# A 192-byte constant tile ahead of three load slots in a decode-attention kernel

## The chip, the core and the metric

The kernel runs on one core of a Trainium2 chip. The metric is the device time of one execution in microseconds. Over three runs it is 684.03 us in the median (683.95 to 684.05).

## The reference

One decode step: eight requests (B = 8), one new token each, model width D = 512. There are 32 query heads, 8 key/value heads and a cache of 4096 positions with 128 elements a head. All data is float32.

```python
xn = _layernorm(x, axis=-1)
...
q = (x @ wq).reshape(B, Sq, Hq, Dh).transpose(0, 2, 1, 3)
scores = jnp.einsum("bhqd,bhkd->bhqk", q, k) * (Dh ** -0.5)
p = _softmax(scores, axis=-1)
o = jnp.einsum("bhqk,bhkd->bhqd", p, v)
s = o.transpose(0, 2, 1, 3).reshape(B, Sq, Hq * Dh) @ wo
...
z = _gelu(jnp.einsum("bsd,df->bsf", x, w_in))
z1 = z[..., :Fh]
z2 = _layernorm(z[..., Fh:], axis=-1)
g = jnp.einsum("ts,bsf->btf", w_sp, z2) + b_sp[None, :, None]
g = _silu(jnp.einsum("bsf,fd->bsd", z1 * g, w_out))
...
return x + s * g
```

In both branches `x` is the normalized `xn`. K and V together are 8 x 8 x 4096 x 128 x 4 x 2 bytes, 268 MB, and each byte is used once; with the weights the kernel reads about 291 MB.

## The kernel before

Everything that is loaded in bulk goes through a **ring of three slots**, the pool `ring` (line 53, `slot()` at line 59). A slot is a tile of 128 partitions x 16384 float32, so 65,536 bytes of each partition and 8 MiB in all. The pools are opened in the order `const`, `ring`, `work`, `small`, and lie in SBUF in this order from low addresses up: first the small constant tiles, then the three slots, then the working tiles `p` and `pT` and the small ones. Where a slot begins therefore depends on how many bytes the constant tiles take.

The order of the work is written out by hand, and one queue, SyncE's (`nc.sync.dma_start`), carries all bulk loads in the order of the program:

- `w_mlp` (L70), the weights of the second branch, 38,912 bytes a partition, into the first slot, with three small pieces of w_out (L75) behind it in the same slot, in 8, 16 and 32 rows;
- `wq` (L86), a whole slot;
- for each of the 8 key/value heads: two loads of K (`load_k`, L313; half the requests each) and two of V (`load_v`, L320), each a whole slot. On the host K and V have been laid out so that each partition's 65,536 bytes are one contiguous run in HBM;
- for the last head, `wo` in seven pieces (L324) into one slot, and the last V in two halves.

A load into a slot waits until the engines are done with what the slot held before and until that earlier load has landed. With three slots, one is being used while two are loaded or wait to be.

The engines do this: `mlp()` computes the second branch into `gate`; `project_q()` (L236) makes the queries, spread with zeros into `qz`; then for each head `scores()` (L258) multiplies the slots with K by `qz` into the PSUM tile `sc`, 64 matmuls of 512 columns a slot; `softmax()` (L263 to L290) makes `pT`; `values()` (L300) multiplies the slots with V, again 64 matmuls a slot, and VectorE (L303, L305) takes the diagonal blocks; `combine()` (L309) gathers the head's output in `oT`. At the end `folded_wo()` (L331) and `direct_wo()` (L338) multiply by wo as its pieces land, two VectorE operations (L382, L383) apply gate and residual, and L384 stores the result, 128 rows of 512 bytes.

Of the kernel before, what the change touches and what calls it, by code (L numbers as in the profile page):

```python
# [8 lines left out]
F32 = mybir.dt.float32  # L9
# [4 lines left out]
P = 128  # L14
# [28 lines left out]
LOW_COLS = 10 * D  # L43
HL_AT = [0, 0, 8]
HL_CH = 10


@with_exitstack
def tile_gqa_gmlp_decode(ctx: ExitStack, tc: tile.TileContext, x, side, kT, v, wq, wo,
                         w_mlp, lows, out):  # L50
    nc = tc.nc
    const = ctx.enter_context(tc.tile_pool(name="const", bufs=1))
# [2 lines left out]
    small = ctx.enter_context(tc.tile_pool(name="small", bufs=2))  # L55
    ps_fix = ctx.enter_context(tc.tile_pool(name="ps_fix", bufs=1, space=bass.MemoryType.PSUM))
    ps = ctx.enter_context(tc.tile_pool(name="ps", bufs=2, space=bass.MemoryType.PSUM))

    def slot():
        return ring.tile([P, SLOT], F32, name="slot")  # L60
# [19 lines left out]
    def from_slot(rows, n):  # L80
        lo = spare[0]
        spare[0] = lo + n
        return mlp_slot[:rows, lo:lo + n]
# [57 lines left out]
    def mlp():  # L141
# [3 lines left out]
        hT = hy[:, :2 * P].rearrange("p (a s) -> p a s", a=2)  # L145
        hL = from_slot(P, HL_CH * P).rearrange("p (a s) -> p a s", s=P)
        y_sb, e = zu[:, :2].rearrange("p a f -> p (a f)"), zu[:, 2, :P]
# [282 lines left out]
```

## Time and profile before

| | |
|---|---|
| time, median of 3 runs | 684.03 us |
| time of the profiled execution | 683.97 us |
| its span, first to last instruction | 682.2 us |
| bytes moved | 291.22 MB in 6445 packets |
| mean rate over the span | 427 GB/s |
| granted TensorE clock, mean | 0.756 of full speed |

Times in the profile are microseconds from the span's start. L258 is line 258 of the kernel before. PE is TensorE's matmuls, PEld its weight loads, DVE VectorE, ACT ScalarE, POOL GpSimd, SP SyncE. The page cuts the span in 40 equal slices: in the row "DMA" each digit is the busy share of the 16 DMA engines in tenths (9 is 90% or more), and "GB/s" is what they moved. A packet is one unit of work of a DMA engine; the row of a queue gives packets, MB, and the packets' time as a share of 16 engines' span. The chain is followed back from the last instruction, at each step to what released it; told in order of time, its columns are start, length, and the work.

### The profile page before, as it was taken

To read this page: it belongs to the slowest core of one execution; us is meant where nothing else is said; L and a number is where in the kernel's file an instruction comes from. 1 tells how busy PE (TensorE), PEld (TensorE's weight loads), DVE (VectorE), ACT (ScalarE), POOL (GpSimd) and SP (SyncE) were. 2 spreads that over 40 slices of the span, in tenths; PEclk is the share of its full clock that TensorE was granted. 3 is DMA by queue.
4 is the path that set the end of the run, shared out by engine and by line. 5 is a ranking of instruction groups with operands and counts; after the bars stand their busy time and mean duration, and the time that the engine had idled before them with its cause. 6 is when DMAs were issued, how large, how long until landed. Compare 5 with 4: busy or idle time off the path is not lost.

```text
span 682.2 us, 5712 instructions
## 1 busy us (share of the span) xinstructions
PE 382.8 (56%) x2610; PEld 117.5 (17%) x2610; DVE 170.5 (25%) x272; ACT 13.5 (2%) x27; POOL 3.9 (1%) x11
## 2 busy tenths in 40 slices
PE   1488454456655355556754465655755356655666
PEld 0222121112111021111211021111211021111212
DVE  2531033401431024401431024401422024400432
ACT  0000000000000000000000000000000000000000
POOL 1000000000000000000000000000000000000000
PEclk9778667878767678887676678877667778876688
DMA  9999999999999999999999999999999999999996
GB/s 384 439 447 432 434 431 430 428 434 428 438 435 430 431 430 435 438 428 430 428 434 443 427 439 439 431 434 431 430 431 430 430 431 428 430 431 434 424 422 263
DMA packets 6445, 291.22 MB, mean 427 GB/s; under 512 B 726, under 2 KB 982, under 8 KB 1534
## 3 DMA queue, kind: packets, MB, share of 16 engines
q1 hardware_dynamic: 6262, 290.79, 98.8%
q8 instruction: 20, 0.33, 0.2%
q10 hardware_dynamic: 160, 0.08, 0.1%
q14 instruction: 3, 0.02, 0.0%
HBM read 290.80 MB, written 0.07 MB: 426 GB/s over the span
## 4 chain that ended last, share of the span: by engine, by line
DMA 79%; PE 16%; issue 4%; DVE 1%; POOLq 0%; POOL 0%
DMA slot<-in_kT 40%; DMA slot<-in_v 28%; DMA slot<-in_wo 10%; PE sc L258 8%; PE o_ps L300 6%; PE sc L215 1%; PE scr L201 0%; PE po_ps L309 0%; DMA x_sb<-in_x 0%; DVE zu L218 0%; DVE st L129 0%; PE scr L191 0%; POOLq L424 0%; POOL rstd L132 0%; PE sc L338 0%
## 5 line engine op out<-in xcount | busy, mean ns | idle before, releaser
L258 PE MATMUL sc<-slot,qz 128*32 128x512 f32 x1024 | 148.0, 743 | 132.1 <-DMA slot<-in_kT 132.1
L300 PE MATMUL o_ps<-slot,pT 128*16 128x512 f32 x1024 | 154.0, 744 | 77.8 <-DMA slot<-in_v 77.8
L303 DVE TENSOR_TENSOR o_all<-o_ps,diag 128x512 f32<-128x512 f32 x64 | 44.2, 691 | 156.7 <-PE o_ps L300 156.3
L263 DVE TENSOR_REDUCE nm<-sc 128x1 f32<-128x1024 f32 x8 | 9.8, 1224 | 278.7 <-PE sc L258 278.7
L258 PEld LDWEIGHTS sc<-slot,qz 128*32 128x32 f32 x1024 | 36.5, 133 | 237.3 <-DMA slot<-in_kT 138.1
L305 DVE TENSOR_REDUCE o_sb<-o_all 128x128 f32<-128x512 f32 x64 | 67.8, 1059 | 2.2
L300 PEld LDWEIGHTS o_ps<-slot,pT 128*16 128x16 f32 x1024 | 30.5, 113 | 161.6 <-issue 106.9
L309 PE MATMUL po_ps<-fold,o_sb 128*128 128x4 f32 x128 | 24.6, 263 | 24.1 <-DVE o_sb L305 23.8
L309 PEld LDWEIGHTS po_ps<-fold,o_sb 128*128 128x128 f32 x128 | 19.0, 188 | 68.8 <-DVE o_sb L305 65.5
L289 PE MATMUL scr<-ident,p 128*128 128x128 f32 x64 | 15.4, 422 | 10.7 <-DVE p L284 10.7
L265 ACT ACTIVATE p<-sc,nm 128x1024 f32<-128x1024 f32 x8 | 8.9, 1113 | 574.5 <-DVE nm L263 574.5
L289 PEld LDWEIGHTS scr<-ident,p 128*128 128x128 f32 x64 | 12.4, 221 | 11.1 <-issue 11.1
L290 DVE COPY pT<-scr 128x512 f32<-128x512 f32 x16 | 11.1, 691 | 11.3 <-PE scr L289 11.3
L155 PE MATMUL scr<-slot,xnT 128*32 128x256 f32 (+1 forms) x64 | 5.2, 464 | 9.5 <-DMA slot<-in_w_mlp 9.5
L236 PE MATMUL scr<-slot,xnT 128*32 128x512 f32 x64 | 9.4, 737 | 0.0
L268 PE MATMUL scr<-ident,nm 128*1 128x128 f32 x8 | 2.2, 270 | 10.9 <-DVE nm L263 10.9
L281 PE MATMUL scr<-wl,same 128*128 128x1 f32 x16 | 3.8, 309 | 6.2 <-DVE wl L279 6.2
L284 DVE TENSOR_SCALAR p<-p,w 128x1024 f32<-128x1024 f32 x8 | 6.0, 753 | 0.3
L331 PE MATMUL sc<-slot,oT 128*8 128x512 f32 x48 | 5.7, 593 | 0.2 <-DMA slot<-in_wo 0.2
L215 PE MATMUL sc<-slot 16*32 16x512 f32 (+2 forms) x36 | 5.3, 664 | 0.8 <-DVE zu L218 0.8
L171 PE MATMUL scr<-part_sum,same 128*128 128x1 f32 x4 | 1.1, 348 | 7.0 <-DVE part_sum L169 7.0
L155 PEld LDWEIGHTS scr<-slot,xnT 128*32 128x32 f32 x64 | 3.0, 141 | 11.3 <-issue 10.8
(87 smaller groups left out, 72.3 us busy)
## 6 DMA issues: line engine op xcount, KB each, us to landing
slot<-in_v SPq DMA_DIRECT2D x2, 4096.0 KB, 26.3
slot<-in_w_mlp SPq DMA_DIRECT2D x1, 4864.0 KB, 14.5
slot<-in_wo SPq DMA_DIRECT2D x1, 3072.0 KB, 36.5
slot<-in_wo SPq DMA_DIRECT2D x1, 2048.0 KB, 40.1
slot<-in_wo SPq DMA_DIRECT2D x1, 1280.0 KB, 42.7
slot<-in_wo SPq DMA_DIRECT2D x1, 768.0 KB
slot<-in_wo SPq DMA_DIRECT2D x1, 512.0 KB
slot<-in_wo SPq DMA_DIRECT2D x2, 256.0 KB, 31.8
```

The lines of the kernel that those rows point to most:

```text
L155: nc.tensor.matmul(pz[R * g:R * (g + 1), part * FQ:part * FQ + n], xnT[:, k, :], w_in_sb[:, k, part * FH + lo:part * FH + lo + n], start=( ...
L215: nc.tensor.matmul(sc[R * g:R * (g + 1), bank, :], lhsT, rhs, start=(i < G), stop=(i + G >= len(part)))
L236: nc.tensor.matmul(pq[R * g:R * (g + 1), :], xnT[:, k, :], wq_sb[:, k, lo:lo + REP * DH], start=(k == 0), stop=(k == NK - 1))
L258: nc.tensor.matmul(sc[R * g:R * (g + 1), c, :], qz[:, h, b * R:(b + 1) * R], k_sb[:, i, c, g, :], start=(b == 0), stop=(b == B - 1))
L263: nc.vector.tensor_reduce(m, sc, op=ALU.max, axis=AX.XY, negate=True)
L265: nc.scalar.activation(p.rearrange("p j s -> p (j s)"), sc.rearrange("p c s -> p (c s)"), AF.Exp, bias=m, accum_out=l[:, h:h + 1])
L289: nc.tensor.transpose(t[:, j * P:(j + 1) * P], p[:, 4 * c + j, :], ident)
L290: nc.vector.tensor_copy(pT[:, :, 4 * c:4 * c + 4].rearrange("p b j (g r) -> p (j g) b r", g=G), t.rearrange("p (m b r) -> p m b r", b=B, r ...
L300: nc.tensor.matmul(of[R * c:R * c + G * REP, :], pT[:, b, j, :], v_unit[:, j], start=(j < G), stop=(j >= J - G))
L303: nc.vector.tensor_mul(o_all, o, diag[:, :, None].to_broadcast([P, G, DH]))
L305: nc.vector.tensor_reduce(o_sb, o_all.rearrange("p g d -> p d g"), op=ALU.add, axis=AX.X)
L309: nc.tensor.matmul(po[:, b * REP:(b + 1) * REP], o_sb, fold, start=True, stop=True)
```

## The change

A constant tile of 128 partitions x 48 float32, 192 bytes a partition, is taken from the pool `const` ahead of all others. Nothing writes or reads it.

```diff
 HL_AT = [0, 0, 8]
 HL_CH = 10
+ALIGN = 48
...
     ps = ctx.enter_context(tc.tile_pool(name="ps", bufs=2, space=bass.MemoryType.PSUM))
+
+    const.tile([P, ALIGN], F32, name="align")
 
     def slot():
         return ring.tile([P, SLOT], F32, name="slot")
```

In the compiled programs the addresses of the tiles within a partition are these (bytes):

| tile | before | after | remainder by 512, before and after |
|---|---|---|---|
| x_sb, the first constant tile | 1152 | 1344 | 128, 320 |
| qz | 4800 | 4992 | 192, 384 |
| res | 16192 | 16384 | 320, 0 |
| first slot | 16704 | 16896 | 320, 0 |
| second slot | 82240 | 82432 | 320, 0 |
| third slot | 147776 | 147968 | 320, 0 |
| pT | 213312 | 213504 | 320, 0 |
| p | 217408 | 217600 | 320, 0 |

All other SBUF tiles of the kernel move by the same 192 bytes. The kernel's lines after the new ones have numbers three higher than before.

## The prediction

> **What bounds the kernel now.** I read the head of the page first, then the DMA lines and the chain that ended last, to see whether any engine matters at all.
>
> ```profile
> span 682.2 us, 5712 instructions
> ...
> PE 382.8 (56%) x2610; PEld 117.5 (17%) x2610; DVE 170.5 (25%) x272; ACT 13.5 (2%) x27; POOL 3.9 (1%) x11
> ...
> DMA  9999999999999999999999999999999999999996
> GB/s 384 439 447 432 434 431 430 428 434 428 438 435 430 431 430 435 438 428 430 428 434 443 427 439 439 431 434 431 430 431 430 430 431 428 430 431 434 424 422 263
> ...
> q1 hardware_dynamic: 6262, 290.79, 98.8%
> ...
> DMA 79%; PE 16%; issue 4%; DVE 1%; POOLq 0%; POOL 0%
> ```
>
> The busiest engine works 56% of the span, while the queue q1, on which SyncE's transfers run, keeps the 16 DMA engines busy for 98.8% of it. The rate is flat from the second slice to the last but one. So the time is the time of moving 290.79 MB. The page's chain gives PE 16% all the same; the chain in order of time, of the middle of the run and of its end, shows why that isn't PE's price:
>
> ```profile
> 78.35 9.60 PE sc L258 x64
> 87.94 0.02 issue
> 87.96 48.40 DMA slot<-in_kT
> 136.36 0.04 issue
> 136.40 9.58 PE sc L258 x64
> 145.99 0.02 issue
> 146.00 48.41 DMA slot<-in_v
> 194.41 0.04 issue
> ...
> 204.89 47.58 DMA slot<-in_v
> 252.47 0.14 issue
> ...
> 262.98 47.54 DMA slot<-in_kT
> 310.52 0.04 issue
> ```
>
> The first column is the start, the second the length. Each time the 64 matmuls on a slot end, the load that was waiting for that slot is issued, and lands 48.4 us later. The landings at the ends of the DMA rows are 136.36, 194.41, 252.47, 310.52: 58.05 us apart, whatever PE did between. The ring has three slots, so three loads of 8 MiB (8,388,608 bytes) land in 58.05 us: **19.35 us a load**, 433.5 GB/s. Of the 48.4 us from issue to landing only 19.35 are the load's own; in the other 29 us it queues behind two earlier loads. PE could give a slot back up to 29 us later and the queue would never run dry. What the chain puts down to PE is hidden behind the other two slots. At the end:
>
> ```profile
> 646.82 31.85 DMA slot<-in_wo
> 678.66 0.04 issue
> 678.71 0.45 PE sc L338 x8
> 679.16 0.02 issue
> 679.18 0.30 DVE res L382
> 679.48 0.02 issue
> 679.51 0.29 DVE res L383
> ```
>
> The last bytes of wo land at 678.66, and 3.5 us of small work and the store of the result follow to the span's end at 682.2. So any change in the time has to come out of the loads, or out of these 3.5 us.
>
> **The change, part by part.** The new tile is never read or written. The two compiled programs hold the same 1855 instructions in the same order on each engine with the same waits, and HBM tensors and PSUM tiles are where they were. Only SBUF addresses differ: all tiles of the kernel move up by 192 bytes. The three slots go from 16704, 82240 and 147776 (each 320 past a multiple of 512, 64 past one of 256) to 16896, 82432 and 147968 (multiples of 512). Nothing changes its distance to another tile. So there is no term for instructions, waits or queues: 0 us each. Two terms are left.
>
> *Engines reading and writing at shifted addresses.* A tile 64-byte-aligned before still is, and one that was not still isn't, since 192 is three times 64. No row shows an operation at both phases, so I bound it: a matmul on a slot could cost more or less, but for 29 us per slot it is covered, which is three times the 9.6 us that PE spends on one. Uncovered are the 0.45 us of L338, and 0.30 and 0.29 us of L382 and L383. If each were a tenth slower or faster, that is 0.1 us. I take 0.
>
> *The loads themselves.* How much of a row's time could depend on where the row starts? The packet counts say what a row is: the 42 big loads (w_mlp, wq, 16 of kT, 17 of v, 7 of wo) and the store have 128 rows each, 5504; the three low pieces of w_out have 8, 16 and 32 rows; that is 5560 of q1's 6262, and the 702 left are the small packets that close a transfer, 16 for each of the 43 (688) and 14 for the low pieces. So **one packet is one row of one partition**, and each of the 16 engines carries 42 x 128 / 16 = 336 rows of the big loads. A row is one contiguous run, so alignment can act at its two ends and otherwise only if every step inside is slower. The DMA lines of two windows tell the two apart, the first (140 to 300 us) of 64 KiB rows, the second (672 to 677 us) of the short rows of wo:
>
> ```profile
> q1 hardware_dynamic: 1183, 69.14, 99.9%
> ```
>
> ```profile
> q1 hardware_dynamic: 460, 1.54, 76.6%
> ```
>
> Packets, MB, share of 16 engines. The first is 0.999 x 160 x 16 = 2557.4 us of engine time, the second 0.766 x 5 x 16 = 61.3 us. With a fixed cost c for each packet and a rate r along it: 2557.4 = 1183 c + 69.14 MB / r and 61.3 = 460 c + 1.54 MB / r. That gives **c = 10 ns** (9.5 to 10.4 with the rounding of the 1.54) and r = 27.16 bytes per ns, 434.6 GB/s for 16 engines. So of a 64 KiB row's 2.42 us all but 10 ns goes at a steady rate.
>
> Alignment's part of the 10 ns is not in this trace, since every big load has the same phase. From above: all of it, 336 x 10 ns = 3.4 us saved, which leaves 680.6. From below: nothing saved, or a loss; I put the end of a loss at the same size, another 10 ns, +3.4 us. The nearest row with another phase at its destination is the store at the end, whose rows of 512 bytes go to an HBM tensor of 512-byte rows (window 680 us to the end, and the issue row):
>
> ```profile
> q1 hardware_dynamic: 144, 0.07, 10.1%
> ...
> out<-res SPq DMA_DIRECT2D x1, 64.0 KB, 1.5
> ```
>
> 0.101 x 2.2 x 16 = 3.56 us; less 65,536 / 27.16 = 2.41 us it leaves 1.14 us for 144 packets, **7.9 ns** a packet. It writes the other way, so it is a neighbour and no measurement; but a fixed cost of 8 ns where the destination starts on 512 leaves 2 ns of the 10 for the phase. I take the middle of 0 and 2 ns: 336 x 1 ns = 0.34 us.
>
> [...]
>
> **The sum.** The profiled execution took 683.97 us with a span of 682.2; the median of the three runs is 684.03 (683.95 to 684.05), 0.06 above it. 683.97 - 0.34 - 0 = **683.6 us**. A measurement of this kernel can tell about 0.2% from no change, 1.4 us, so this is no change: the limits are 682.66 and 685.40. In rows, 1.37 us / 336 = 4.1 ns: alignment has to be worth four of the ten nanoseconds to be seen.
>
> **Rivals.**
>
> *Faster: most of the fixed cost is the phase.* A row that starts and ends inside a block of 256 or 512 bytes might cost one whole extra block, 256 / 27.16 = 9.4 ns, nearly the whole 10. That would give 336 x 9.4 = 3.2 us, 680.8; the case begins at 4.1 ns and 682.6 and ends at 680.6. For it: 10 ns is just of that size. Against it: the store has 7.9 ns without that phase, and the rate along a row is the same for long and short rows, so nothing is lost inside them. [...]
>
> *Slower: writes collide with reads in SBUF.* Slots, p and pT now all start on a multiple of 512, and matmuls read the slots in blocks of 2 KiB. If a row's write that begins on such a boundary had to wait for a read of the same phase, each row would cost more; from 4.1 ns a row it shows, and doubled (another 10 ns) it is 687.4. The place is every load beside which PE runs. Four equal stretches say how much the loads feel of PE now:
>
> ```profile
> 100.00:225.00 125.00, 69.05 (x484) 20.11 (x476) 32.81 (x44) 1.41 (x3) 0.00 (x0) 0.77 1.00 431
> 225.00:350.00 125.00, 66.29 (x436) 20.38 (x440) 30.12 (x45) 2.81 (x6) 0.00 (x0) 0.74 1.00 433
> 350.00:475.00 125.00, 72.68 (x484) 20.40 (x476) 26.55 (x37) 1.41 (x3) 0.00 (x0) 0.73 1.01 435
> 475.00:600.00 125.00, 68.54 (x440) 21.29 (x440) 36.67 (x54) 2.81 (x6) 0.00 (x0) 0.75 0.99 429
> ```
>
> The third column is PE's busy time, the last GB/s. The stretch with the busiest PE, 72.68 us, has the best rate, 435; the others scatter by the packets that fall on their edges. That speaks against a collision, and so does that all distances between tiles stay. What can't be excluded is a phase that only now arises.
>
> *It does nothing at all.* The slots do move as said, but a row of 64 KiB may be long enough for its ends to be lost: 684.0. This lies inside the forecast's case.
>
> **How the numbers follow.** No change (0 to 4 ns a row gained, or up to 4 lost): 0.70. Faster: 0.18; slower: 0.12. These are also the chances of the three classes. The no-change case reaches from 682.66 to 685.40. For 8 in 10 another 0.10 is wanted; I take it from the nearer part of the faster case, as that has the larger chance: 7 ns a row, 336 x 7 = 2.35 us, 681.6. Left out are its far part, 0.08, and the slower case, 0.12. Range 681.6 to 685.4.
>
> **What the profile afterwards would show.** The count of instructions stays 5712, q1 keeps 6262 packets and 290.79 MB. Three landings in the chain are 24 rows per engine: with 1 ns a row 58.05 us becomes 58.03, with all 10 ns 57.81, in the slower case 58.15 to 58.29. PE's busy time can move with the granted clock without any effect. The last landing moves from 678.66 by the sum, with 3.5 us behind it. What would make me wrong: a landing distance under 57.95 or over 58.15, a rate that changes inside the rows, or a new idle time of q1.

## The result and the profile after

| | before | after |
|---|---|---|
| median | 683.98 us (683.80 to 684.12, 19 runs) | 682.66 us (682.52 to 682.87, 19 runs) |
| profiled execution | 683.97 us, span 682.2 | 682.87 us, span 681.1 |

The ratio is 0.9981, with a 95% interval of 0.9974 to 0.9988: 1.32 us faster, and clear of no change. The forecast was 683.6 in a range of 681.6 to 685.4, with "no change" likeliest, which the prediction let end at 682.66, 0.2% below the time before. The direction and the range hold. The measured median lies exactly on that end, so that it falls into the likeliest case is luck; the gain is four times the 0.34 us of the sum.

The page of the changed kernel, the lines that answer to those of before:

```profile
span 681.1 us, 5712 instructions
...
PE 377.8 (55%) x2610; PEld 116.2 (17%) x2610; DVE 170.5 (25%) x272; ACT 13.5 (2%) x27; POOL 4.0 (1%) x11
...
q1 hardware_dynamic: 6262, 290.79, 98.8%
...
DMA 76%; PE 18%; issue 4%; DVE 2%; POOLq 0%; POOL 0%; SPq 0%
```

Instructions, packets and bytes are as before, and q1 fills the same 98.8% of a shorter span. PE's 5 us less busy time are no cause: queueing still covers it, as 28.5 to 29.7 of the 47.84 to 49.00 us from issue to landing below are not the 19.32 of the load itself. The chain in order of time (start, length, work), first of the changed kernel:

```profile
107.47 47.89 DMA slot<-in_kT
...
164.32 49.00 DMA slot<-in_kT
...
222.31 48.97 DMA slot<-in_v
...
281.29 47.97 DMA slot<-in_v
...
571.18 47.84 DMA slot<-in_kT
```

and of the kernel before the last row of the same kind, which the prediction didn't need:

```profile
552.28 48.52 DMA slot<-in_kT
```

Start plus length is a landing. After: 155.36, 213.32, 271.28, 329.26, and 619.02 as the ninth, so (619.02 - 155.36) / 8 = **57.96 us** for three loads. Before, from 136.36 to 552.28 + 48.52 = 600.80: 464.44 / 8 = **58.055**. The 0.097 us between them are 24 rows an engine, **4.0 ns a row**. The end of the chain:

```profile
628.64 36.33 DMA slot<-in_v
664.97 0.04 issue
665.01 6.59 PE o_ps L303 x32
...
677.35 0.70 PE sc L341 x24
678.07 0.30 DVE res L385
678.40 0.29 DVE res L386
```

Lines are three higher than before. From the first of the two VectorE operations to the span's end it is 3.0 us in both (682.2 - 679.18; 681.1 - 678.07), so the gain was made ahead of it. This one profiled execution shows 1.1 us of the 1.32; at 682.87 it is the slowest of the 19. Its chain shows why it fell short: it ends with PE's work on the last half slot of V, and no matmul at L341 waits for wo any more, where the last one of L338 did before. The 32 matmuls at 665.01 took 6.59 us, the same 32 of the kernel before 5.32. Here the work behind the last V, and not the landing of wo, set the end.

### The profile page after: what moved, and what is told of

Read it like the earlier page. It is cut to its first block, busy times and chain, and to the rows that moved or that the text cites. A ratio compares the mean times of both kernels' runs of the same rounds, so it can differ in the third digit from the quotient of the medians.

```text
span 681.1 us, 5712 instructions
## 1 busy us (share of the span) xinstructions
PE 377.8 (55%) x2610; PEld 116.2 (17%) x2610; DVE 170.5 (25%) x272; ACT 13.5 (2%) x27; POOL 4.0 (1%) x11
## 3 DMA queue, kind: packets, MB, share of 16 engines
q1 hardware_dynamic: 6262, 290.79, 98.8%
## 4 chain that ended last, share of the span: by engine, by line
DMA 76%; PE 18%; issue 4%; DVE 2%; POOLq 0%; POOL 0%; SPq 0%
DMA slot<-in_v 40%; DMA slot<-in_kT 35%; PE o_ps L303 7%; PE sc L261 7%; PE scr L239 1%; PE sc L218 1%; PE po_ps L312 1%; PE scr L204 0%; DVE o_sb L308 0%; PE sc L334 0%; DMA x_sb<-in_x 0%; DVE o_all L306 0%; PE sc L341 0%; DVE q_sb L242 0%; DVE zu L221 0%
## 5 line engine op out<-in xcount | busy, mean ns | idle before, releaser
L261 PE MATMUL sc<-slot,qz 128*32 128x512 f32 x1024 | 143.9, 725 | 132.5 <-DMA slot<-in_kT 132.5
```

The lines of the kernel that those rows point to most:

```text
L261: nc.tensor.matmul(sc[R * g:R * (g + 1), c, :], qz[:, h, b * R:(b + 1) * R], k_sb[:, i, c, g, :], start=(b == 0), stop=(b == B - 1))
```

## The experiments

Theory: a row of a load pays a price when its write begins inside a 256-byte block of SBUF, whatever the row's length; the runs below show 3.4 to 5.1 ns. (Nearly all rows here are multiples of 256 bytes long, so a row that begins inside a block also ends inside one; no run tells the two ends apart.) Its rivals blame the moved constant or working tiles, blocks of 512 bytes, a loss along the whole row, a collision with PE's reads, or the place of the row's source relative to its destination. All medians are of 11 runs, except for the pair with four loads a slot, of 4 and 5; the kernel before ran beside them, in 21 to 33 runs, at 683.95 to 684.00.

### Which of the moved tiles

`slots_alone` takes the tile last from the constant pool:

```diff
-    const.tile([P, ALIGN], F32, name="align")
...
     res = const.tile([P, P], F32, name="res")
+    const.tile([P, ALIGN], F32, name="align")
```

> The 192-byte tile is taken last from the constant pool, so the constant tiles stay where they were before, and slots and working tiles move as in the change. Theory A (the start of a load's row in the slot decides): as the change, 682.7. Theory B (the moved constant tiles that the engines read, qz above all, decide): 684.0 as before.

Measured: 682.74 (ratio 0.9982, 0.9973 to 0.9991). `work_alone` takes it from the working pool:

```diff
-    const.tile([P, ALIGN], F32, name="align")
+    work.tile([P, ALIGN], F32, name="align")
```

> The 192-byte tile is taken from the working pool instead: p, pT and the small tiles move, slots and constant tiles stay where they were before. Theory A (the start of a load's row in the slot decides): 684.0 as before. Theory C (the working tiles decide, by what the engines read and write there): 682.7 as the change.

Measured: 684.01 (1.0000, 0.9991 to 1.0009). With the constant tiles back in place the whole gain stays; with p and pT moved and the slots in place nothing of it is there. B and C fall: it is the slots.

### How large a block

Four kernels differ from the change in one number, the width of the tile, and so in where the slots begin.

```diff
-ALIGN = 48
+ALIGN = 112   # r256
+ALIGN = 104   # r224
+ALIGN = 56    # r32
+ALIGN = 80    # r128
```

> The tile has 448 bytes, so that slots start 256 past a multiple of 512. Theory A1 (blocks of 256 bytes): as the change, 682.7. Theory A2 (blocks of 512 bytes): as before, 684.0.

> The tile has 416 bytes, so that slots start 224 past a multiple of 512, where before they were 64 past one of 256. [...] Theory A1b (one fixed cost for each row that does not start on a block): as before, 684.0.

> The tile has 224 bytes, so that slots start 32 past a multiple of 512. Theory F (one fixed price for a row that starts inside a block of 256 bytes): 684.0, as with 64 past. Theory G (a price that grows with the bytes ahead of the start, drawn through 64 past at 684.0 and 224 past at 684.35): 683.9. Theory H (the row's smallest piece decides, 32 bytes here at its end as with 224 past at its start): 684.35.

> The tile has 320 bytes, so that slots start 128 past a multiple of 256. Theory F: 684.0. Theory G: 684.1 to 684.2. Theory H (the pieces at both ends have 128 bytes, the largest that both can have): 684.0 or less.

| start of a slot, past a multiple of 256 | kernel | median, us | above the change, per row | three landings, us | mean 64 KiB row, ns |
|---|---|---|---|---|---|
| 0 (and 0 past 512) | the change | 682.66 | 0 | 57.958 | 2420.7 |
| 0 (and 256 past 512) | r256 | 682.69 | 0.1 ns | 57.976 | 2420.8 |
| 128 | r128 | 683.80 | 3.4 ns | 58.048 | 2423.8 |
| 64 | before | 683.98 | 3.9 ns | 58.055 | 2424.0 |
| 32 | r32 | 684.37 | 5.1 ns | 58.080 | 2424.9 |
| 224 | r224 | 684.35 | 5.0 ns | 58.079 | 2424.9 |

The fourth column is the difference of the medians over 336 rows. r256 has a ratio of 0.9981 (0.9972 to 0.9990): the block is of 256 bytes, not the 512 that the change aims at. The landings show the same. First r256, then r224, r32 and r128:

```profile
87.08 48.96 DMA slot<-in_kT
...
551.10 48.75 DMA slot<-in_kT
```

```profile
88.14 48.28 DMA slot<-in_kT
...
552.57 48.48 DMA slot<-in_kT
```

```profile
87.27 49.06 DMA slot<-in_kT
...
551.69 49.28 DMA slot<-in_kT
```

```profile
107.75 47.96 DMA slot<-in_kT
...
572.14 47.95 DMA slot<-in_kT
```

Eight distances each: for r256 (599.85 - 136.04) / 8 = 57.98 us, of which the first is 58.09 and the other seven are 57.96 in the mean; for r224 (601.05 - 136.42) / 8 = 58.08 us; r32 and r128 likewise. The last column is the mean over the 4096 rows of 64 KiB, from the time that the trace records for each packet; these differ a little less than the landings do (3.3 ns against 4.0 for the kernel before), and where the rest lies was not traced.

Theory G, a price that grows with the bytes ahead of the start, expected 683.9 for r32 and 684.1 to 684.2 for r128 and falls: they got 684.37 and 683.80, and 32 and 224 past cost the same, 5.1 and 5.0 ns a row. Most of it is there for every start inside a block (A1b, which expected 684.0 for r224 and got 684.35). The rest goes as theory H has it: 5 ns where the smallest piece of the row has 32 bytes, 3.9 for 64, 3.4 for 128. That ladder is finer than the intervals against before (r32 1.0006, 0.9997 to 1.0015; r128 0.9997, 0.9988 to 1.0006). It rests on the runs themselves, 684.10 to 684.56 for r32 and 683.64 to 683.92 for r128, which do not overlap, and on the landings and the rows of the traces, which fall in the same order. The step from 128 to 64 is the weakest: the runs of these two kernels overlap.

The price is a mean. In the change 3986 of the 4096 rows took 2418 ns. Before, 529 did; the most frequent time was 2420 ns, in 1964 rows, and 745 took 2427. Why some rows pay 2 ns and others 9, and why a smaller piece costs more, was not tried: the records show how long a row took, not what the DMA engine did at its ends.

### Per row or per byte

Both kernels load each slot of K and V by four loads; one has the slots of before, the other those of the change.

```diff
-        nc.sync.dma_start(t, kT[h, half])
+        n = SLOT // 4
+        for c in range(4):
+            nc.sync.dma_start(t[:, c * n:(c + 1) * n], kT[h, half][:, c * n:(c + 1) * n])
...
-                v_sb = load_v(h, half, 2)
+                v_sb = load_v(h, half, 4)
...
-                v_sb = load_v(h, half, 1)
+                v_sb = load_v(h, half, 4)
```

> Each load of K and V is issued as four loads of 16 KiB rows, with slots where they were before. To be compared with split4_after. Theory R (a price per row for its two ends): 1.32 us / 336 rows is 3.9 ns, and now there are 1096 rows an engine, so the two differ by 4.3 us. Theory L (a loss spread over the bytes of a row): the bytes are the same, so the two differ by 1.3 us as before. In both the additional rows cost their fixed part, 760 x about 6 to 10 ns, 4.6 to 7.6 us, on top of 684.

> Four loads of 16 KiB rows for each load of K and V, with slots on multiples of 512 as in the change. Theory R: 4.3 us below split4_before. Theory L: 1.3 us below it.

Measured: 691.47 (ratio 1.0112, 1.0098 to 1.0126; runs of 691.34 to 691.93) and 687.13 (1.0053, 1.0040 to 1.0065; 686.71 to 688.71), 4.34 us apart. Theory R expected 4.3, theory L 1.3; even the runs that lie closest are 2.6 us apart. The chain of each, first with the slots of before:

```profile
78.84 39.14 DMA slot<-in_v
...
587.87 39.15 DMA slot<-in_kT
```

```profile
92.91 38.88 DMA slot<-in_kT
...
598.59 38.88 DMA slot<-in_v
```

One link now spans two slots, 64 rows of 16 KiB an engine. Over 13 links it is (587.87 - 78.84) / 13 = 39.16 us from start to start against (598.59 - 92.91) / 13 = 38.90, 0.26 us or 4.0 ns a row, the same as for rows of 64 KiB. The pair also splits the fixed cost. Four loads for one add 760 rows an engine: 687.13 - 682.66 = 4.47 us or **5.9 ns a row** on the block border, 691.47 - 683.98 = 7.49 us or **9.9 ns a row** inside it. The links, free of the spread of these few runs, give 5.4 and 9.4 (two thirds of 57.96 and 58.055 us taken off, over 48 rows). Each includes a row's share of the small packets that close the 95 loads more: q1 has 19,942 packets in split4_before against 6262, and of the 13,680 more 95 x 128 = 12,160 are rows and 1520, 16 a load, are these.

### Does PE's reading matter

```diff
     def scores(h, half, k_sb):
-        for i in range(HALF):
+        if half == 0:
+            return
+        for i in range(HALF - 1, HALF):
...
-        for j in range(J):
+        for j in range(G):
...
-                o_sb = values(b, pT, v_sb[:, i])
+                o_sb = o_prev if i else values(b, pT, v_sb[:, i])
```

(The start and stop flags of the matmuls that stay follow from this.)

> Of the matmuls on the slots with K and V only 16 of 256 for each head are kept, 8 on K and 8 on V (the rest of scores and values is left out, so the output is another one), with slots where they were before. All loads stay. To be compared with quiet_after. Theory R (the price is paid within the load): still 1.3 us above quiet_after. Theory P (writes that start inside a block collide with PE's reads of the slots): nearly nothing to collide with, under 0.2 us above it. The time itself stays near 684, as the loads bound it.

> The same 16 of 256 matmuls a head, with slots on multiples of 512 as in the change. Theory R: 1.3 us below quiet_before, near 682.7. Theory P: within 0.2 us of quiet_before.

Measured: 684.22 (684.03 to 684.74) and 683.05 (682.68 to 683.75), 1.17 us apart. The page of quiet_before shows how little is left to collide with, and that the loads bind as ever:

```profile
PE 154.0 (23%) x818; PEld 68.4 (10%) x818; DVE 86.0 (13%) x176; ACT 13.5 (2%) x27; POOL 3.9 (1%) x11
...
q1 hardware_dynamic: 6262, 290.79, 98.7%
...
L260 PE MATMUL sc<-slot,qz 128*32 128x512 f32 x128 | 28.4, 1037 | 252.3 <-DMA slot<-in_kT 252.3
L302 PE MATMUL o_ps<-slot,pT 128*16 128x512 f32 x128 | 30.5, 1046 | 170.8 <-DMA slot<-in_v 170.8
```

The profile lists each matmul call as two instructions: 128 each at L260 and L302 instead of 1024. So what is kept is an eighth, 16 of 128 calls a head; the 256 of the expectation were instructions. Nine tenths of the difference are still there. Theory P expected under 0.2 us and falls. Whether the last 0.15 us belong to the reads is not settled: they are less than the spread of either kernel's runs. The mean 64 KiB row takes 2422.5 and 2419.1 ns in the two traces, 3.4 apart, where it is 3.3 with all matmuls; without the few rows (under 2%) that took over 15 ns more than the median it is 3.0 and 3.4.

### Source or destination

Rows of K and V begin 320 bytes later in HBM, with rows 66,048 bytes apart, once into the slots of before and once into those of the change.

```diff
+PAD, ROW = 80, SLOT + 128
...
-        nc.sync.dma_start(t, kT[h, half])
+        nc.sync.dma_start(t, kT[h, half][:, PAD:PAD + SLOT])
...
-            nc.sync.dma_start(t[:, c * n:(c + 1) * n], v[h, half][:, c * n:(c + 1) * n])
+            nc.sync.dma_start(t[:, c * n:(c + 1) * n], v[h, half][:, PAD + c * n:PAD + (c + 1) * n])
...
```

> The rows of K and V in HBM get 320 bytes of zeros ahead and 192 behind, so that the loads read from 320 past a multiple of 512, into slots that start 320 past one as before. 264 of the 336 rows an engine are concerned, 1.03 us at 3.9 ns. Theory S (a row pays when source and destination start at different places of a block): 1.0 us below before, 683.0, and below src320_dst0. Theory W (only where the write starts decides): 684.0 as before. Theory E (each side pays for its own start): 685.0. The rows now lie 66,048 bytes apart in HBM, which may move this and src320_dst0 alike.

> The same source, 320 past a multiple of 512, into slots on multiples of 512 as in the change. Theory S: as before, 683.7 to 684.0, and above src320_dst320. Theory W: as the change, 682.7, 1.3 us below src320_dst320. Theory E: 683.7, also 1.3 us below src320_dst320.

Measured: 683.93 (ratio 0.9999, 0.9990 to 1.0008) and 682.59 (0.9979, 0.9970 to 0.9988): theory W. Theory S expected 683.0 for the first and theory E 685.0, and both fall. The chains, first src320_dst320:

```profile
88.31 48.13 DMA slot<-in_kT
...
552.63 48.24 DMA slot<-in_kT
```

```profile
86.78 49.37 DMA slot<-in_kT
...
550.71 49.09 DMA slot<-in_kT
```

464.43 / 8 = 58.05 us and 463.65 / 8 = 57.96 us, the two distances of before and after. A source 320 bytes further on costs nothing, and doesn't make up for a destination that is off. The offset counts from the start of the HBM tensor, and no run shows where that lies; if it lies inside a block itself, a price that is the same for every start inside one would not show here.

## Why the prediction was right, and where it was short

- **The bound.** Right: the loads carry the time. quiet_before does an eighth of the matmuls on K and V and takes 684.22, for 683.98 before.
- **No term for instructions, waits and queues; 0 for the engines at shifted addresses.** Right in size: work_alone moves p and pT and stays at 684.01 (that 64 bytes are a step that matters to an engine no run shows), and the end from the first of the two last VectorE operations on is 3.0 us in both profiles. But the list of uncovered work was too short. The 29 us of queueing cover PE as long as loads are queued, and behind the last ones none are: in the profile afterwards the end hangs on PE's work on the last half slot of V, 6.59 us for its 32 matmuls, not on wo.
- **One packet is one row, with a fixed cost of 10 ns, and nothing is lost along a row.** Right, and measured apart from the fit: 7.49 us for the 760 rows and 95 closing packets that are added on each engine to the kernel before, 8.8 ns a packet as the fit counts them or 9.9 ns a row, and 4.0 ns of difference for rows of 16 KiB as for 64 KiB.
- **Alignment's part of the 10 ns, taken as 1 ns.** This is the step that was short: it is 3.9 ns (1.32 us / 336; the interval of the ratio allows 2.4 to 5.3), with 5.4 to 5.9 left on the border. The 1 ns came from the store's 7.9 ns, as half of the 2 ns that this left. The store was the nearest row and the wrong ruler: it writes to HBM, and its 7.9 ns a packet are not the fixed cost of an aligned load, which by 4.47 us for 855 packets more is 5.2. The bounds of 0 and 10 held, and the estimate sat too near the lower one. With the 4.0 ns of the landings the sum is 683.97 - 1.34 = 682.63.
- **Faster, as a rival.** A whole extra block of 9.4 ns a row is excluded: the most that any start cost is 5.1. The saving stopped just short of the border of this case, 4.1 ns, and within its interval could lie on either side.
- **Slower by a collision.** Nothing of it: aligned starts were faster, with all of PE's reads (682.66 for 683.98) and with an eighth of them (683.05 for 684.22).
- **The signs named beforehand.** 58.03 us between three landings was expected, under 57.95 would have been wrong; it is 57.96, less than half a nanosecond a row away from that. Instructions, packets and bytes stayed, as named.

## What to carry over

In a kernel whose loads fill the DMA engines nearly all the time (98.8% of the span here), look at where each row begins within its partition: a start inside a 256-byte block costs 3.4 to 5.1 ns a row here in the mean, and as much for rows of 16 KiB as of 64 KiB where that was tried (4.0 ns in both). It is 0.19% for rows of 64 KiB and 0.6% (4.34 of 691.47 us) when they are cut to 16 KiB, so it is worth a padding tile and more worth it for short rows; making the rows long buys more (4.5 to 7.5 us here). Bound such a price by a pair of windows with long and short rows, and take a neighbouring row that goes the other way only as a bound. When the loads get shorter, look again at the end of the run: the work behind the last load has no slack of queued loads to hide in (6.59 us of matmuls on the last half slot of V in the profile afterwards, where they took 5.32 before).

## What the hardware did that was not expected

- The write side counts: a source moved by 320 bytes left both kernels where they were (683.93 for 683.98 before, 682.59 for 682.66 after the change).
- The price is nearly flat in the place of the start (3.4 ns at 128 past a block's border, 5.0 at 224) and goes rather with the smaller of the two pieces at the row's ends: 32 and 224 past are equal (5.1 and 5.0). It is a mean of unequal rows: at 64 past half of them take 2 ns more than the 2418 that nearly all take on the border, and nearly a quarter 7 or 9 more.
- With an eighth of the matmuls on K and V (quiet_before), the mean granted clock of TensorE was 0.551 for 0.756 before, and a matmul at L260 took 1037 ns against 743 at L258 of the kernel before; the time stayed the same (684.22 for 683.98).
